# Both feed-forward products of pairs of token blocks as seven block products (Strassen) instead of eight

## The chip, the cores and the metric

The kernel runs on one core of a Trainium2 chip. Its time is the device time of one execution, in microseconds; a profile of one further execution shows what each engine did. The engines are TensorE (PE, with weight loads on PEld), VectorE (DVE), ScalarE (ACT), GpSimd (POOL) and SyncE (SP), which here issues nearly all DMA transfers. Each engine works through its own instructions in order, and waits on semaphores for the others.

## The reference

Attention with heads mixed before and after the softmax, then a feed-forward layer with the gate h - tanh(h):

```
scores = scale * np.matmul(q, k.transpose(0, 1, 3, 2))      # 8 x 12 x 448 x 448
scores = np.einsum('bhij,hg->bgij', scores, w_pre)
scores = scores - np.max(scores, axis=-1, keepdims=True)
attn = np.exp(scores)
attn = attn / (np.sum(attn, axis=-1, keepdims=True) + 1e-09)
attn = np.einsum('bhij,hg->bgij', attn, w_post)
x = np.matmul(attn, v)        # heads side by side: 3584 tokens x 768
h = x @ w_in                  # 768 x 2048
g = h - np.tanh(h)
return (g @ w_out).astype(np.float32)      # 2048 x 768
```

The weights w_in and w_out arrive as 8-byte floats.

## The kernel before

**Precision.** A product of float32 matrices is made of three matmuls in fp32r: each operand is split into a high part (the cast) and a low part (the difference), and high by high, high by low and low by high are summed in PSUM.

**Attention** (until about 854 us) goes through 180 places. A place gathers two groups of rows of scores, mixes them with w_pre (`premix`, L521), takes the maximum (DVE, L530) and the exponential (ACT, L532), and scales the post-mixing weights by the sums (`norm`: DVE L541 and L542, then POOL L543 into the tile wr). The matmuls of `mix` (L560), a place later, wait for wr. Scores, transposes and values of other rows are fitted in between by a table of due places. A generator, `narrow_steps`, adds some steps of weight conversion to each place: `narrow_chunk` (L71 to L110) turns 8-byte floats into high and low parts with operations on DVE, ACT and POOL (L96, L98, L104) and stores them in DRAM (ws). The steps are spread evenly over the places, so that POOL has the wr of each place and one or two operations of conversion between.

**Feed-forward.** The 3584 tokens are 7 blocks of 512. A block has 16 chunks of 128 hidden features. For a chunk, `hidden` multiplies 6 slices of 128 of x by w_in in 18 matmuls of 512 columns (L257, L258, L262) into one PSUM bank; `gate` and `parts_gate` make the gate from it with four passes on ACT and six on DVE, and a cast and a difference for its parts; `result` multiplies the parts by the chunk's rows of w_out, for 4 groups of 128 tokens, in 12 matmuls of 512 columns (tile ya) and 12 of 256 (yb), which add up over the 16 chunks in six banks. `hidden` of the next chunk is issued ahead of `result` of the current one, so that PE has work while the gate is made. One DMA of 1.5 MB a chunk brings the weights (tile w, a ring of six, `load_w`), and x of the next block is loaded and split during the current one, a slice every other chunk, the low part on POOL (L247).

**Order.** `in_order` chains the instructions of each engine in the order in which the program emits them. Nothing is reordered later.

## Time and profile before

| | |
|---|---|
| time, median of 3 (lowest to highest) | 1781.2 us (1780.5 to 1787.9) |
| span of the profiled execution, first to last instruction | 1783.2 us |
| attention, until about | 854 us |
| feed-forward, the rest | 929 us |
| PE / DVE / ACT / POOL busy, share of the span | 98 / 63 / 56 / 18% |
| bytes moved by DMA, mean rate | 372 MB, 209 GB/s |
| granted TensorE clock | 0.995 |

The profile gives no time of the profiled execution but its span. Busy times of matmuls overlap (the next one starts before the last has drained), so a matmul's cost is read from the distance between starts. In the groups, the number behind "idle" is the time for which the engine stood still just before these instructions, and what ended it.

### The profile page before, as it was taken

The numbers are of one execution on the slowest core, as the hardware profiler recorded it, in microseconds if no ns is written. First come the engines' busy times: TensorE is split into PE (matmuls) and PEld (weight loads), VectorE is DVE, ScalarE is ACT, GpSimd is POOL, SyncE is SP. The second block draws the span as 40 slices with busy tenths as digits, with TensorE's granted clock in tenths as the row PEclk, the third lists the DMA queues.
The fourth block names the chain that finished last, engine by engine and source line by source line (L and its number), as shares of the span: only waits on it lengthen the run. The fifth ranks groups of instructions, "written<-read, shape, count | busy, mean of one in ns | idle before, by whom it ended". The sixth has DMA issues, their size and how long they took to land.

```text
span 1783.2 us, 41383 instructions
## 1 busy us (share of the span) xinstructions
PE 1749.8 (98%) x16572; PEld 1421.2 (80%) x16572; DVE 1127.6 (63%) x2362; ACT 998.9 (56%) x2051; POOL 321.1 (18%) x417
## 2 busy tenths in 40 slices
...
GB/s 182 205 193 225 193 239 220 216 211 206 235 214 211 214 213 227 189 203 221 270 193 209 239 193 215 229 200 213 224 208 205 229 213 197 237 212 188 233 192 36
DMA packets 232816, 372.32 MB, mean 209 GB/s; under 512 B 98992, under 2 KB 207536, under 8 KB 218288
## 3 DMA queue, kind: packets, MB, share of 16 engines
...
q14 instruction: 61, 0.50, 0.1%
HBM read 245.37 MB, written 47.19 MB: 164 GB/s over the span
## 4 chain that ended last, share of the span: by engine, by line
PE 84%; DMA 5%; ACT 3%; DVE 3%; SPq 2%; issue 1%; POOL 1%; ACTq 0%; POOLq 0%; DVEq 0%
PE ps_o L560 12%; PE ps_h L257 8%; PE ps_h L258 8%; PE ps_h L262 8%; PE ps_m L602 7%; PE ps_p L521 7%; PE ya L305 6%; PE ya L302 6%; PE ya L303 6%; PE ps_q L477 5%; PE yb L305 3%; PE yb L303 3%; PE yb L302 3%; DMA t<-s 2%; SPq L369 1%
## 5 line engine op out<-in xcount | busy, mean ns | idle before, releaser
L560 PEld LDWEIGHTS ps_o<-wr,e 60*112 60x112 f32 (+1 forms) x5760 | 305.3, 175 | 34.3 <-POOL wr L543 17.2
L560 PE MATMUL ps_o<-wr,e 60*112 60x60 f32 (+1 forms) x5760 | 313.8, 258 | 8.8 <-POOL wr L543 6.7
L530 DVE TENSOR_REDUCE mx<-ps_p 128x1 f32<-128x448 f32 x360 | 207.7, 619 | 167.1 <-PE ps_p L521 166.6
L532 ACT ACTIVATE e<-ps_p,mx 128x448 f32<-128x448 f32 x360 | 225.7, 634 | 103.0 <-DVE mx L530 101.2
L289 ACT CAST gh<-r 128x512 fp32r<-128x512 f32 x112 | 69.5, 621 | 372.7 <-DVE r L282 372.7
L257 PE MATMUL ps_h<-xh,w 128*128 128x512 f32 x672 | 263.9, 393 | 0.0
L258 PE MATMUL ps_h<-xl,w 128*128 128x512 f32 x672 | 263.7, 392 | 0.0
L570 ACT COPY at<-ps_o 112x960 f32<-112x960 f32 x156 | 154.0, 987 | 92.0 <-PE ps_o L560 91.8
L521 PE MATMUL ps_p<-t,wpre 60*64 60x448 f32 (+1 forms) x1440 | 180.2, 568 | 7.7 <-DMA t<-s 7.7
L247 POOL TENSOR_TENSOR xl<-rx,xh 128x512 fp32r<-128x512 f32 x38 | 56.3, 1483 | 728.8 <-ACT xh L246 728.8
L278 DVE SCALAR_TENSOR_TENSOR r<-qa,ps_h 128x512 f32<-128x512 f32 x112 | 77.1, 689 | 158.8 <-ACT t L275 158.8
L305 PE MATMUL ya<-w,gl 128*128 128x512 f32 x448 | 176.7, 394 | 0.7 <-DVE gl L290 0.7
L302 PE MATMUL ya<-w,gh 128*128 128x512 f32 x448 | 174.9, 390 | 1.0 <-ACT gh L289 1.0
L303 PE MATMUL ya<-w,gh 128*128 128x512 f32 x448 | 174.7, 390 | 0.0
L602 PEld LDWEIGHTS ps_m<-at,vr 112*64 112x64 f32 x3072 | 147.9, 137 | 30.2 <-ACT at L577 10.4
L262 PE MATMUL ps_h<-xh,w 128*128 128x512 f32 x672 | 170.5, 389 | 0.0
L602 PE MATMUL ps_m<-at,vr 112*64 112x120 f32 (+1 forms) x3072 | 162.1, 262 | 7.4 <-ACT at L577 2.9
L272 ACT ACTIVATE u<-ps_h 128x512 f32<-128x512 f32 x112 | 67.0, 599 | 151.1 <-PE ps_h L262 151.1
L262 PEld LDWEIGHTS ps_h<-xh,w 128*128 128x128 f32 x672 | 126.1, 188 | 26.2
L258 PEld LDWEIGHTS ps_h<-xl,w 128*128 128x128 f32 x672 | 127.2, 189 | 23.6
L257 PEld LDWEIGHTS ps_h<-xh,w 128*128 128x128 f32 x672 | 127.2, 189 | 23.3
L543 POOL TENSOR_TENSOR wr<-wpost,zs 128x120 f32<-128x120 f32 x180 | 70.3, 391 | 401.3 <-DVE zs L542 302.6
...
## 6 DMA issues: line engine op xcount, KB each, us to landing
w<-ws SPq DMA_DIRECT2D x112, 1536.0 KB
...
```

The source lines that it names most:

```text
L257: nc.tensor.matmul(ph, wh[:, fs], xh, start=(c == 0), stop=False)
L258: nc.tensor.matmul(ph, wh[:, fs], xl, start=False, stop=False)
L262: nc.tensor.matmul(ph, wl[:, fs], xh, start=False, stop=(c == NK - 1))
L302: nc.tensor.matmul(y, gh[:, tok], wh[:, es], start=first, stop=False)
L303: nc.tensor.matmul(y, gh[:, tok], wl[:, es], start=False, stop=False)
L305: nc.tensor.matmul(y, gl[:, tok], wh[:, es], start=False, stop=last)
L521: nc.tensor.matmul(pss[r][halves[j], :], wpre[k, :], ts[j][k, :], start=True, stop=True)
L530: nc.vector.tensor_reduce(out=mx, in_=ps, axis=AX.X, op=ALU.max, negate=True)
L532: nc.scalar.activation(e, ps, AF.Exp, bias=mx, scale=1.0, accum_out=zs[:, 0, r : r + 1])
L560: nc.tensor.matmul(ps[:CP, j, c * GP : (c + 1) * GP].rearrange("p (h i) -> p h i", i=GI)[:, :, r * GH : (r + 1) * GH], e[k, c * CP : (c + ...
L570: nc.scalar.copy(ats[i0][:, :, :, at : at + 2 * GI].rearrange("p c h (j i) -> p j (c h) i", j=2), ps[:CP, :, : NC * GP].rearrange("p j (x ...
L602: nc.tensor.matmul(pv[j * D : (j + 1) * D, r, :n], vt[:, j, c, :], ats[i][:, c, 2 * hp + j, :n], start=(c == 0), stop=(c == NC - 1),)
```

## The change

Block 0 is computed as before. Blocks 1 to 6 are taken in three pairs, and both products of a pair are made by Strassen's scheme in Winograd's form: each matrix is cut into four quarters, and seven products of quarters (or of their sums) replace eight.

* **Weights.** `narrow_quad` converts four quarters at a time (4 x 128 columns) and also makes four sums of them: `sums_in` for w_in, `sums_out` for w_out, on POOL and one on ACT. High and low parts of quarters (wi, wo) and of sums (ss, ts) are stored in DRAM. POOL has four operations of 512 columns, and four of 128 (or one of 256 and two of 128) per quad; there are 48 quads.
* **Block 0.** `Block0.step` makes one hidden product, 18 matmuls as before; its PSUM bank is copied to SBUF by ACT, and the gate works on two chunks at once (1024 columns). The gates of block 0 are stored in DRAM (go) and read back for the result.
* **Hidden products of a pair.** `pair_step` runs eight times per pair, each for two chunks of both blocks: seven products of 9 matmuls of 512 columns, alternately in two PSUM banks X and Y. Products 2, 4 and 6 go on adding in X, and 5 in Y, with copies and sums between them on ACT and DVE (into h01 and h23). From these come two gates of 1024 columns and, a step late (`Late`), the sums of gates; one store of 7 x 512 columns (gs) puts them in DRAM.
* **Results of a pair** are made while the next pair's hidden products run. `Results` is a generator of units of 12 matmuls: for block 0 two groups of tokens as before; for a pair, one of seven products with 384 columns, which reads a gate sum from DRAM (`more_gr`), splits it (`parts`: a cast on ACT, a difference on DVE) and multiplies it by weight tiles (`more_w2`), each two or three ahead. Each step of pair 1 has 3 units, each step of pairs 2 and 3 has 5 or 6. Between two pairs stand 12 units, and after the last pair all that are left.
* **x of a pair.** Five raw quarters are loaded (`load_xq`), in the last step of the pair before; `xq_jobs` makes their four sums and all high and low parts, on ACT and DVE, 1536 columns at a time: nine jobs, for pair 1 during block 0, and for the others one with each unit between the pairs.
* The six-slot weight ring, `hidden`, `gate`, `parts_x`, `result` and the finishing functions are gone, and POOL has no work in the feed-forward but two low parts of block 0's x.

The diff, cut:

```diff
+    nc.scalar.copy(oh, m)
+    t = pool.tile([p, 4, 2, 128], F32, name="ct", tag="ct", bufs=2)
+    for job in sums(nc, m, t[:, :, 1]):
+        yield "step"
+    nc.gpsimd.tensor_sub(ol, m, raw(oh))
     yield "step"
-    nc.gpsimd.tensor_sub(fl, m, raw(fh))
+    nc.scalar.copy(t[:, :, 0].bitcast(F32R), t[:, :, 1])
+    dma(dst, raw(o).rearrange("p x t n -> p x (t n)"))
     yield "step"
-    for to, part in zip(dst, (fh, fl)):
-        if len(to.shape) == 3:
-            part = part.rearrange("p (f n) -> p f n", f=to.shape[1])
-        dma(to, raw(part))
+    nc.gpsimd.tensor_sub(t[:, :, 1].bitcast(F32R), t[:, :, 1], t[:, :, 0])
     yield "step"
+    dma(sums_dst, t.rearrange("p s t n -> p s (t n)"))
+    yield "step"
+def sums_in(nc, m, t):
+    a11, a12, a21, a22 = [m[:, x] for x in range(4)]
+    s2, s1, s3, s4 = [t[:, x] for x in range(4)]
+    nc.gpsimd.tensor_tensor(out=s1, in0=a21, in1=a22, op=ALU.add)
+    yield
+    nc.gpsimd.tensor_tensor(out=s2, in0=s1, in1=a11, op=ALU.subtract)
+    yield
+    nc.gpsimd.tensor_tensor(out=s3, in0=a11, in1=a21, op=ALU.subtract)
+    yield
+    nc.gpsimd.tensor_tensor(out=s4, in0=a12, in1=s2, op=ALU.subtract)
+    yield
+def sums_out(nc, m, t):
+    b11, b12, b21 = [m[:, x] for x in range(3)]
+    t1, t2, t3, t4 = [t[:, x] for x in (0, 1, 3, 2)]
+    both = b12.unsqueeze(1).to_broadcast([b12.shape[0], 2, b12.shape[1]])
+    nc.gpsimd.tensor_tensor(out=t[:, 0:4:3], in0=m[:, 0:4:3], in1=both, op=ALU.subtract)
+    yield
+    nc.gpsimd.tensor_tensor(out=t2, in0=b11, in1=t3, op=ALU.add)
+    yield
+    nc.gpsimd.tensor_tensor(out=t4, in0=t2, in1=b21, op=ALU.subtract)
+    yield
+    nc.scalar.mul(t2, t2, -1.0)
...
+    def load_w0(f):
+        w = ff.w0.tile([P, NK, 2, P], F32R, name="w0", tag="w0")
+        nc.sync.dma_start(raw(w), wis[f // 2][:, f % 2])
+        ff.w[f] = w
+    def products(ph, w, xs, start, stop):
+        n = len(xs)
+        for c, (xh, xl) in enumerate(xs):
+            nc.tensor.matmul(ph, w[:, c, 0], xh, start=start and c == 0, stop=False, skip_group_check=True)
+            nc.tensor.matmul(ph, w[:, c, 0], xl, start=False, stop=False, skip_group_check=True)
+        for c, (xh, _) in enumerate(xs):
+            nc.tensor.matmul(ph, w[:, c, 1], xh, start=False, stop=stop and c == n - 1, skip_group_check=True)
...
+        def a1(self):
+            self.u, self.qa = work("u"), work("qa")
+            nc.scalar.activation(self.u, self.h, AF.Square)
+            nc.scalar.activation(self.qa, self.u, AF.Square, bias=ff.bias[:, 0:1], scale=GATE_A[0])
+        def a2(self):
+            self.qb, self.t = work("qb"), work("t")
+            nc.scalar.activation(self.t, self.h, AF.Tanh)
+            nc.scalar.activation(self.qb, self.u, AF.Square, bias=ff.bias[:, 1:2], scale=GATE_B[0])
+        def d1(self):
+            nc.vector.scalar_tensor_tensor(out=self.qa, in0=self.qa, scalar=GATE_A[2], in1=self.h, op0=ALU.add, op1=ALU.mult)
+            nc.vector.tensor_sub(self.t, self.h, self.t)
+        def d2(self):
+            nc.vector.scalar_tensor_tensor(out=self.qa, in0=self.qb, scalar=GATE_B[2], in1=self.qa, op0=ALU.add, op1=ALU.mult)
+        def a3(self):
+            nc.scalar.activation(self.qb, self.u, AF.Relu, bias=ff.bias[:, 2:3], scale=1.0)
+        def d3(self, out):
+            nc.vector.tensor_mul(out, self.qa, self.u)
+            nc.vector.copy_predicated(out, self.qb.bitcast(I32), self.t)
...
+        def step(self):
+            f, old = self.f, self.old
+            self.f += 1
+            if f + 2 < NF:
+                load_w0(f + 2)
+            if f < NF:
+                ph = hbank()
+                products(ph, ff.w.pop(f), [ff.x[c] for c in range(NK)], True, True)
+                if f % 2 == 0:
+                    self.h = work(("h01", "h23")[f // 2 % 2])
+                nc.scalar.copy(self.h[:, f % 2], ph)
+            if f % 2:
+                if old:
+                    old.d2()
+                    old.a3()
+                    g = work("g", 7)[:, :2]
+                    old.d3(g)
+                    nc.sync.dma_start(gos[:, f - 3 : f - 1], g)
+                self.old = Gate(self.h) if f < NF else None
+            elif old:
+                old.a1()
+                old.a2()
+                old.d1()
...
+        def parts(self, n):
+            if n < len(self.items) and n == self.n_parts:
+                lo = ff.gr.pop(n)
+                hi = ff.gph.tile([P, 2, TB], F32R, name="gh", tag="gh")
+                nc.scalar.copy(hi, raw(lo))
+                nc.vector.tensor_sub(lo, raw(lo), raw(hi))
+                ff.gp[n] = hi, lo
+                self.n_parts += 1
...
+            first, last = new and k0 + k == 0, k0 + k == NQ - 1
+            for t in range(NT):
+                tok, y = slice(t * TT, (t + 1) * TT), self.y[t][:, :N2]
+                nc.tensor.matmul(y, gh[:, tok], wh, start=first, stop=False, skip_group_check=True)
+                nc.tensor.matmul(y, gh[:, tok], wl, start=False, stop=False, skip_group_check=True)
+                nc.tensor.matmul(y, gl[:, tok], wh, start=False, stop=last, skip_group_check=True)
...
+        def sub(x, y):
+            nc.vector.tensor_sub(xr, x if x is xr else raw(ff.xs[x]), y if y is xr else raw(ff.xs[y]))
+        def high(x, src):
+            x_tiles(x + "h")
+            nc.scalar.copy(ff.xs[x + "h"], src)
+        def low(x, src):
+            nc.vector.tensor_sub(ff.xs[x + "l"], src, raw(ff.xs[x + "h"]))
+        def both(x):
+            high(x, raw(ff.xs[x + "l"]))
+            low(x, raw(ff.xs[x + "l"]))
+        xr = ff.xr.tile([P, HK, TB], F32, name="xr", tag="xr")
+        sub("t3l", "b11l")
+        both("b11")
+        yield
+        x_tiles("t1l")
+        high("t1", xr)
+        both("b21")
+        yield
+        low("t1", xr)
+        sub("b22l", xr)
+        yield
+        x_tiles("t2l")
+        high("t2", xr)
+        low("t2", xr)
+        yield
+        sub("t4l", xr)
+        yield
+        high("t4", xr)
+        low("t4", xr)
+        yield
+        sub("b22l", "t3l")
+        yield
+        high("t3", xr)
+        low("t3", xr)
+        yield
+        both("b22")
...
+        def v0(self):
+            self.g = work("g", 7)
+            self.g2.a1()
+            self.g1.d3(self.g[:, 0:2])
+        def v1(self):
+            self.g2.a2()
+        def v2(self):
+            self.g2.d1()
+            self.g2.d2()
+        def v3(self):
+            g = self.g
+            self.g2.a3()
+            self.g2.d3(g[:, 2:4])
+            nc.vector.tensor_add(g[:, 4:6], g[:, 0:2], g[:, 2].unsqueeze(1).to_broadcast([P, 2, TB]))
+        def v4(self):
+            g = self.g
+            nc.vector.tensor_add(g[:, 6], g[:, 1], g[:, 4])
+            nc.vector.tensor_add(g[:, 2], g[:, 3], g[:, 6])
+            nc.sync.dma_start(gss[self.s][:, :, self.q], g)
+            ff.stored[self.s] = self.q + 1
...
+        X, Y = hbank(), hbank()
+        product(0, X, True)
+        h01 = work("h01")
+        nc.scalar.copy(h01[:, 1], X)
+        if late:
+            late.v0()
+        rest(0)
+        product(1, Y, True)
+        nc.vector.tensor_add(h01[:, 1], Y, h01[:, 1])
+        if late:
+            late.v1()
+        rest(1)
+        product(2, X, False)
+        if late:
+            late.v2()
+        h23 = work("h23")
+        nc.scalar.mul(h23[:, 0], X, -1.0)
+        rest(2)
+        product(3, Y, True)
+        if late:
+            late.v3()
+        nc.scalar.mul(h01[:, 0], Y, -1.0)
+        rest(3)
+        product(4, X, False)
+        nc.vector.tensor_sub(h01[:, 0], h01[:, 0], X)
+        if late:
+            late.v4()
+        g1 = Gate(h01)
+        g1.a1()
+        rest(4)
+        product(5, Y, False)
+        nc.vector.tensor_sub(h23[:, 0], h23[:, 0], Y)
+        g1.a2()
+        g1.d1()
+        rest(5)
+        product(6, X, False)
+        nc.scalar.copy(h23[:, 1], X)
+        g1.d2()
+        g1.a3()
...
+    load_all_xq(0, ("b11l", "b21l", "t3l", "b22l", "t4l"))
-    for n in range(N):
-        b, f = n // NF, n % NF
-        if n + ahead < N:
-            load_w(n + ahead)
...
+    while block0.f < NF + 2:
+        block0.step()
+        if 3 <= block0.f < NF + 1 and block0.f % 2:
+            next(xq, None)
+        if block0.f == NF - 2:
+            res.more_w2(1)
+        if block0.f == NF:
+            close_plain()
+            more_wa(6)
...
+    HELD, AHEAD = 8, 4
+    late, left = None, 4 * NQ
+    for s in range(NS):
+        per_step = (left - HELD) / NQ
+        due = 0.0
+        for p in range(NQ):
+            def between(i):
+                next(xq, None)
+                if p == NQ - 1 and s + 1 < NS:
+                    for x, at in (("b11l", 0), ("b21l", 1), ("t3l", 4), ("b22l", 5), ("t4l", 6)):
+                        if i == at:
+                            load_all_xq(s + 1, (x,))
+            units = []
+            for i in range(7):
+                due += per_step / 7
+                units.append(int(due))
+                due -= int(due)
+            late = pair_step(s, p, late, units, between)
+        left = 7 * NQ - AHEAD
+        if s + 1 < NS:
+            xq = xq_jobs()
+        for f in (late.v0, late.v1, late.v2, late.v3, late.v4):
+            f()
+            next(xq, None)
+            res.units(1)
+        late = None
+        if s + 1 < NS:
+            for _ in range(HELD + AHEAD - 5):
+                next(xq, None)
+                res.units(1)
+    for _ in res.at:
+        pass
```

428 lines of the change are left out of this document (264 added, 164 removed).

## The prediction

> **What bounds the kernel now.** I read the page's first table, then the busy time by stretches (columns: stretch and its length, then busy us and, in brackets, instructions of PE, PEld, DVE, ACT, POOL; last the granted clock, the DMA share and GB/s), cut where attention ends.
>
> ```profile
> span 1783.2 us, 41383 instructions
> ...
> PE 1749.8 (98%) x16572; PEld 1421.2 (80%) x16572; DVE 1127.6 (63%) x2362; ACT 998.9 (56%) x2051; POOL 321.1 (18%) x417
> ```
>
> ```profile
> 0.00:854.00 854.00, 826.81 (x11897) 637.93 (x11898) 586.94 (x1577) 619.02 (x1408) 267.47 (x381) 0.99 0.73 210
> 854.00:1783.00 929.00, 923.02 (x4676) 783.31 (x4675) 540.68 (x786) 379.92 (x644) 53.65 (x36) 1.00 0.58 208
> ```
>
> From 854 us on PE is busy 923 of 929 us at full clock, DVE 58% of the time, ACT 41%: the feed-forward is bound by matmuls and has room elsewhere. Before 854 us PE idles 27 us, with DVE at 69% and ACT at 72%. So matmuls taken from the second stretch shorten it, as long as the others keep up.
>
> Busy times of matmuls overlap, so their price is read from starts in order of time (start, us, what):
>
> ```profile
> 889.83 0.39 PE L302 MATMUL ya<-w,gh 128*128 128x512 f32 x1
> ...
> 892.32 0.39 PE L305 MATMUL ya<-w,gl 128*128 128x512 f32 x1
> ...
> 892.55 0.28 PE L302 MATMUL yb<-w,gh 128*128 128x256 f32 x1
> ...
> 893.86 0.28 PE L305 MATMUL yb<-w,gl 128*128 128x256 f32 x1
> ...
> 893.98 0.40 PE L257 MATMUL ps_h<-xh,w 128*128 128x512 f32 x1
> ...
> 896.50 0.39 PE L258 MATMUL ps_h<-xl,w 128*128 128x512 f32 x1
> ...
> 896.73 1.52 PE L262 MATMUL ps_h<-xh,w 128*128 128x512 f32 x6
> ...
> 898.35 0.60 ACT L272 ACTIVATE u<-ps_h 128x512 f32<-128x512 f32 x1 [0.64 <-PE ps_h L262]
> ```
>
> Each pair of rows is the first and last of 12 matmuls, 11 intervals: 2.49/11 = 0.226 us (512 columns, result), 1.31/11 = 0.119 us (256 columns), 2.52/11 = 0.229 us (512 columns, hidden). A chunk is 18 x 0.229 + 12 x 0.226 + 12 x 0.119 = 8.26 us.
>
> **What the change saves on PE.** Block 0 keeps its matmuls. A pair had 2 x 16 x 18 = 576 hidden matmuls and gets 8 steps x 7 products x 9 = 504 of the same size: 72 x 0.229 = 16.5 us, three pairs 49.5 us. Its result had 384 matmuls of 512 and 384 of 256 columns, 132.5 us; now 7 x 8 x 4 x 3 = 672 of 384 columns. No row has 384; on the line between the two it is 0.173 us (bounds 0.119 and 0.226), so 116.3 us: 16.2 us a pair, 48.7 us for three. Together **-98.2 us**.
>
> **Elementwise prices.** The gate now works on 1024 columns and the x parts on 1536; neither is in the trace. Groups of instructions (count | busy us, mean ns | idle before):
>
> ```profile
> L289 ACT CAST gh<-r 128x512 fp32r<-128x512 f32 x112 | 69.5, 621 | 372.7 <-DVE r L282 372.7
> L570 ACT COPY at<-ps_o 112x960 f32<-112x960 f32 x156 | 154.0, 987 | 92.0 <-PE ps_o L560 91.8
> L290 DVE TENSOR_TENSOR gl<-r,gh 128x512 fp32r<-128x512 f32 x112 | 78.6, 702 | 77.6 <-ACT gh L289 77.6
> L280 DVE TENSOR_TENSOR r<-r,u 128x512 f32<-128x512 f32 x112 | 109.0, 973 | 3.8
> L247 DVE TENSOR_TENSOR xl<-rx,xh 128x512 fp32r<-128x512 f32 x4 | 2.6, 684 | 1.1 <-ACT xh L246 1.1
> L429 DVE TENSOR_TENSOR kk<-ps_k,kk 128x448 fp32r<-128x448 f32 x2 | 1.1, 616 | 0.0
> ```
>
> DVE: (684 - 616)/64 = 1.06 ns a column, so 1.23 us for 1024 and 1.77 us for 1536. ACT: (987 - 621)/448 = 0.82 ns, so 1.04 and 1.46 us. L280 is dearer than its like; in order of time:
>
> ```profile
> 893.50 1.64 POOL L247 TENSOR_TENSOR xl<-rx,xh 128x512 fp32r<-128x512 f32 x1 [12.23 <-ACT xh L246]
> ...
> 894.02 1.66 DVE L280 TENSOR_TENSOR r<-r,u 128x512 f32<-128x512 f32 x1
> ```
>
> It ends 0.54 us after POOL's, so about 0.7 us of it are its own work: beside POOL it is held up. The new feed-forward gives POOL nothing to do, so I use the undisturbed price. The Trainium skill (SBUF — State Buffer, "SBUF: two separate sides") gives this as a lock: a DVE operation with two SBUF inputs and a GpSimd one that reads SBUF exclude each other for the whole instruction. The trace agrees with the row above; with L280's 0.97 us for all two-input work the next term would be some 28 us larger.
>
> **The gaps between pairs: +48 us.** In a step of pair 1 PE has 63 x 0.229 = 14.4 us of hidden and 3 units of result (12 matmuls, 2.08 us each): 20.7 us; in pairs 2 and 3 5.5 units, 25.9 us. DVE per step: two gates of 5 operations of 1024 (12.3), gate sums 1 of 1024 and 2 of 512 (2.6), three PSUM sums (2.1), parts of stored gates 0.75 to 2.75 x 1.23 (0.9 to 3.4): 18 to 20.4 us. It fits. Between two pairs, though, PE has 12 units, 25 us, while DVE must finish the last gates and make the next pair's x parts. Before, x came a chunk at a time, on POOL. DVE, one whole chunk of the feed-forward before (far, r, t are gate tiles, gl the low part of the finished gate):
>
> ```order
> L277 TENSOR_SCALAR far<-u 128x512
> L278 SCALAR_TENSOR_TENSOR r<-qa,ps_h 128x512
> L279 SCALAR_TENSOR_TENSOR r<-qb,r 128x512
> L280 TENSOR_TENSOR r<-r,u 128x512
> L281 TENSOR_TENSOR t<-ps_h,t 128x512
> L282 COPY_PREDICATED r<-far,t 128x512
> L290 TENSOR_TENSOR gl<-r,gh 128x512
> ```
>
> and now, the second half of the first gap (g is the tile of gates and their sums; b, t and xr are parts of x; gl a gate read back for the result, the last row those of the last units):
>
> ```order
> L638 TENSOR_TENSOR g<-g 128x1024
> L568 TENSOR_TENSOR t2l<-xr,t2h 128x1536
> L642 TENSOR_TENSOR g<-g 128x512
> L643 TENSOR_TENSOR g<-g 128x512
> L561 TENSOR_TENSOR xr<-t4l,xr 128x1536
> L438 TENSOR_TENSOR gl<-gl,gh 128x1024
> L568 TENSOR_TENSOR t4l<-xr,t4h 128x1536
> L561 TENSOR_TENSOR xr<-b22l,t3l 128x1536
> L568 TENSOR_TENSOR t3l<-xr,t3h 128x1536
> L568 TENSOR_TENSOR b22l<-b22l,b22h 128x1536
> L438 TENSOR_TENSOR gl<-gl,gh 128x1024 x2
> ```
>
> What moved: a whole pair's x parts now stand ahead of the gate parts that PE waits for. Counted from the gap's start there are 11 of 1536 (19.5 us), 11 of 1024 up to the first of the last two (13.5) and 2 of 512 (1.4): 34.4 us, against 10 units = 20.8 us on PE, so PE waits 13.6 us. On ACT the high parts (7 x 1.46 us) stand in line with Squares and Tanh, and DVE's next row needs them: the one for b21 comes some 3 us late, the four differences each cost up to 1.5: I add 8, 22 us. The second gap has two parts and eight sums more, 2.5 + 8 x 0.55 = 7 on DVE, some of it inside ACT's waits: 26 us. Bounds: 34 (no wait for ACT) and 70 (every cast waited for, 2 x 7 x 1.46, and handovers).
>
> **Other stalls in the feed-forward.** (a) Pair 1's x, 3.9 MB, is now issued on SP ahead of hidden product 3's weights:
>
> ```profile
> 851.42 0.50 PE L257 MATMUL ps_h<-xh,w 128*128 128x512 f32 x1
> 854.89 0.57 SPq L369 DMA_DIRECT2D xs<-x  x1
> 859.78 0.40 PE L257 MATMUL ps_h<-xh,w 128*128 128x512 f32 x1
> ```
>
> SP where attention's last output goes out, before (w_N is one feature chunk's weights, xs_N attention's output, rx raw x):
>
> ```order
> L369 DMA xs_64<-x 768x1x208
> L334 DMA w_13209<-ws_65 128x3072
> L334 DMA w_13211<-ws_66 128x3072
> L334 DMA w_13213<-ws_66 128x3072
> L334 DMA w_13284<-ws_66 128x3072
> L334 DMA w_13349<-ws_66 128x3072
> L238 DMA rx<-xs_58 128x384
> ```
>
> and now (b11l to t4l are the five raw quarters of pair 1's x, the last row the weights of hidden product 3):
>
> ```order
> L738 DMA xs_64<-x 768x1x208
> L556 DMA b11l<-xs_58 128x3x384
> L556 DMA b11l<-xs_59 128x3x128
> L556 DMA b21l<-xs_58 128x3x384
> L556 DMA b21l<-xs_59 128x3x128
> L556 DMA t3l<-xs_59 128x3x320
> L556 DMA t3l<-xs_60 128x3x192
> L556 DMA b22l<-xs_59 128x3x320
> L556 DMA b22l<-xs_60 128x3x192
> L556 DMA t4l<-xs_58 128x3x384
> L556 DMA t4l<-xs_59 128x3x128
> L308 DMA w_13433<-wi_66 128x1536
> ```
>
> What moved: ten x transfers got between the last output and those weights, which were in SBUF or first in line before. And product 3 comes sooner, with hidden products 1 and 2 alone ahead of it: 851.4 + 2 x 4.1 = 859.7. The DMA rows by stretch of one chunk:
>
> ```profile
> 866.25:874.50 8.25, 8.25 (x44) 7.06 (x43) 4.53 (x7) 3.03 (x6) 0.00 (x0) 1.00 1.01 426
> 899.25:907.50 8.25, 8.25 (x43) 7.06 (x42) 4.49 (x8) 2.97 (x6) 0.00 (x0) 1.00 0.52 186
> 400.00:500.00 100.00, 98.11 (x1456) 76.22 (x1454) 73.15 (x196) 76.57 (x174) 34.94 (x44) 1.00 0.80 225
> ```
>
> The saturated rate is 426 GB/s: 4.7 MB take 11 us from 854.9, so PE waits **6 us** (0 if attention's end leaves SP free sooner, 12 at 281 GB/s). The Trainium skill (DMA: Bandwidth & Descriptors, "Where 436 GB/s comes from") has about 358 GB/s of HBM as the limit of a core; the row is above it. By that page this would be 13 us, the stall 8.
>
> (b) Pair 1's first weights are loaded over block 0's last ones, so PE waits for one whole DMA of 0.39 MB; the nearest row, of the chain of waits (start, us), is of a 0.2 MB one:
>
> ```profile
> 21.95 3.53 DMA t<-s
> ```
>
> I take 3.5 us (bounds 1, at 426 GB/s, and 8). (c) In pairs 2 and 3 three steps each end without a result unit, and the next product reuses the PSUM bank just filled: a copy like L272, from 898.35 to 898.95, where the next matmul would start at 898.1: 1.0 us x 6 = 6 us. (d) Block 0: DVE needs 5 x 1.23 + 19.5/7 = 8.9 us per two products of 8.2 on PE: 5 us; waits of the single gate-sum tile for its store, closings of products: 3. Together 8 (0 to 35, the latter if that store holds each step of pair 1 for 4 us).
>
> Transfers otherwise hide: a step of pairs 2 and 3 moves 7 weight tiles of 0.39 MB, 1.84 MB of gates to DRAM, and 2.75 times 0.79 MB of weights and 0.52 MB of gates back, 8.2 MB in 25.9 us or 317 GB/s; a step of pair 1 6.2 MB in 20.7 us.
>
> **Attention: +12 us.** POOL rows (by form), and PE's wait:
>
> ```profile
> L98 POOL TENSOR_TENSOR cm<-cm,cr 128x512 f32<-128x512 f32 x24 | 31.8, 1325 | 0.7
> L543 POOL TENSOR_TENSOR wr<-wpost,zs 128x120 f32<-128x120 f32 x180 | 70.3, 391 | 401.3 <-DVE zs L542 302.6 <-PE ps_o L560 49.0 <-PE ps_p L521 19.7
> L560 PEld LDWEIGHTS ps_o<-wr,e 60*112 60x112 f32 (+1 forms) x5760 | 305.3, 175 | 34.3 <-POOL wr L543 17.2 <-issue 8.6 <-POOL cl L104 1.3
> ```
>
> POOL in the middle of attention before (wr is what each mix on PE waits for, the others convert weights):
>
> ```order
> L543 TENSOR_TENSOR wr<-wpost,zs 128x2x60
> L96 TENSOR_TENSOR cm<-cr,cs 128x512
> L98 TENSOR_TENSOR cm<-cm,cr 128x512
> L543 TENSOR_TENSOR wr<-wpost,zs 128x2x60
> L104 TENSOR_TENSOR cl<-cm,cs 128x512
> ```
>
> and now (co the parts of a weight, ct those of its sums):
>
> ```order
> L912 TENSOR_TENSOR wr<-wpost,zs 128x2x60
> L97 TENSOR_TENSOR cm<-cr,co 128x512
> L110 TENSOR_TENSOR ct<-ct 128x4x128
> L99 TENSOR_TENSOR cm<-cm,cr 128x512
> L912 TENSOR_TENSOR wr<-wpost,zs 128x2x60
> L120 TENSOR_TENSOR ct<-cm 128x128
> L122 TENSOR_TENSOR ct<-ct,cm 128x128
> L124 TENSOR_TENSOR ct<-cm 128x128
> L126 TENSOR_TENSOR ct<-cm,ct 128x128
> ```
>
> What moved: up to four conversions, where one or two stood, are ahead of a wr. They cost POOL 192 us before (56 x 3 operations); now 48 x 4 x 1.3 + about 48 x 1.6 for the sums = 327, +135. 854 us in 180 places is 4.7 us a place, and 0.4 + 2.0 us fit; but rows like L110 wait for ACT and hold wr. PE's 17 us for wr, scaled by 327/192, become 29: +12. Bounds 0 and 68, half of what is added.
>
> **Sum.** -98.2 + 48 + 6 + 3.5 + 6 + 8 + 12 = -14.7: the profiled 1783.2 becomes 1768.5. The shown median, 1781.2, lies 2.0 below that execution, so **1766**; 1745 to 1800 if this account holds.
>
> **Rivals.** A: DVE is no limit in the gaps, and POOL no limit before: without those 60 us, 1706. For it: DVE 58% busy. Against: the 34 us counted. B, slower: POOL in order holds wr. Its price is half the added 135 us, 68 instead of 12: 1822. It decides where a place's POOL rows outlast the place: the one quoted has 0.4 + 3.9 us of 4.7, plus waits. Against: most wr wait for zs now (303 of 401 us). C: transfers get only attention's rate, 225/0.80 = 281 GB/s; late steps then take 29.2 us, 16 x 3.3 = 53, pair 1's 8 x 1.3 = 10, and the closing results (1.31 MB per 4.16 us of PE) 30 x 0.5 = 15: 1844. Against: 426 was reached; for it: 1 to 3 KB rows.
>
> **Chances.** Forecast 0.55, A 0.17, B 0.16, C 0.12. This kernel's measurement tells about 0.5% (1772 to 1790) from no change. Faster: A and two thirds of the forecast, 0.53; same 0.18; slower: B, C and a little, 0.29. The range 1708 to 1818 leaves out C and the ends of A and B.
>
> **What would show it.** PE idle of 15 to 30 us twice, some 200 us apart, ended by DVE's gl; an idle of about 6 us four products into the feed-forward, ended by a weight DMA; hidden and result spacing unchanged, 0.17 us for 384 columns; POOL near 410 us, PE's wait for wr near 30. Wrong if PE is full in the gaps (A), if the first stretch passes 900 us (B), or the DMA share sits at 1.0 through the late steps (C).

## The result: 3% slower

The changed kernel takes 1837.0 us (median of 4, 1836.7 to 1841.2) against 1783.6 for the kernel before beside it: a ratio of 1.031 (95% interval 1.028 to 1.035). Forecast were 1766 and a range of 1708 to 1818; the time lies outside, on the other side of 1781.

Busy time by stretches, the changed kernel's profile first. The columns are those of the prediction's first such view; the cuts are, in order, attention, block 0, pair 1, gap 1, pair 2, gap 2, pair 3 and the rest (the "tail"):

```profile
0.00:870.30 870.30, 826.72 (x11773) 636.98 (x11773) 583.59 (x1530) 644.06 (x1449) 402.46 (x572) 0.98 0.79 232
870.30:986.30 116.00, 80.52 (x387) 64.23 (x385) 63.53 (x52) 57.52 (x63) 1.51 (x3) 0.82 0.52 180
986.30:1160.30 174.00, 167.99 (x781) 139.25 (x782) 132.80 (x128) 105.52 (x115) 0.00 (x0) 0.97 0.78 283
1160.30:1214.00 53.70, 32.98 (x156) 29.49 (x155) 36.88 (x27) 24.74 (x31) 0.00 (x0) 0.81 0.79 281
1214.00:1420.80 206.80, 206.80 (x1024) 185.35 (x1023) 148.49 (x144) 123.43 (x143) 0.00 (x0) 1.00 0.86 314
1420.80:1471.50 50.70, 30.70 (x144) 28.38 (x143) 40.23 (x35) 21.84 (x19) 0.00 (x0) 0.83 0.79 281
1471.50:1678.30 206.80, 206.80 (x1024) 185.35 (x1023) 147.97 (x143) 123.18 (x143) 0.00 (x0) 1.00 0.82 301
1678.30:1839.40 161.10, 144.12 (x792) 141.76 (x791) 61.97 (x64) 47.76 (x55) 0.00 (x0) 0.96 0.85 303
```

The kernel before, cut where its feed-forward starts, which is at about 842 us and not at the 854 that stand ahead of the prediction:

```profile
0.00:842.20 842.20, 815.01 (x11773) 628.05 (x11774) 582.74 (x1570) 615.25 (x1401) 264.89 (x379) 0.99 0.74 211
842.20:1783.20 941.00, 934.82 (x4800) 793.19 (x4799) 544.88 (x793) 383.69 (x651) 56.23 (x39) 1.00 0.57 207
```

Pairs 2 and 3 are what was forecast: 206.8 us for 8 steps, 25.85 a step, TensorE (PE) never idle, full clock. Everything between is not. Block 0 has 288 matmuls of 0.229 us, 66 us (with 96 small ones of attention's end the stretch comes to 70), and takes 116. And the granted clock, the last but two number, is 0.81 to 0.83 in block 0 and the gaps and 0.96 to 0.98 in attention, pair 1 and the tail; before the change it was 1.00 through the feed-forward.

So each stretch has three parts: matmuls at full speed, idle time, and what the half clock costs. The last I work out from the trace's records as half of the time in which PE was busy while the granted clock stood at 0.5.

| us | length | idle | lost at half clock | full speed |
|---|---|---|---|---|
| before: attention | 841.8 | 27.2 | 6.9 | 807.7 |
| before: feed-forward | 941.4 | 6.2 | 1.6 | 933.6 |
| after: attention | 870.3 | 43.6 | 17.4 | 809.3 |
| after: feed-forward | 969.2 | 99.2 | 29.8 | 840.2 |
| of it block 0 | 116.0 | 35.5 | 10.3 | 70.2 |
| pair 1 | 174.0 | 6.0 | 3.9 | 164.1 |
| the two gaps | 104.5 | 40.7 | 10.0 | 53.8 |
| tail | 161.2 | 17.0 | 5.5 | 138.6 |

The scheme's saving is there: 933.6 to 840.2, 93.4 us. It is eaten by 93.0 us of new idle and 28.2 us of half clock in the feed-forward, and attention adds 28.5. Where the five longest idles of PE in the feed-forward ended (PE in order of time; the bracket gives the idle before the row and what ended it):

```profile
898.58 0.77 PE L315 MATMUL ps_h<-xh,w 128*128 128x512 f32 x1 [10.17 <-DMA w<-wi]
...
928.90 0.77 PE L315 MATMUL ps_h<-xh,w 128*128 128x512 f32 x1 [5.88 <-DMA w<-wi]
...
986.27 0.76 PE L315 MATMUL ps_h<-b11h,wa 128*128 128x512 f32 x1 [13.49 <-DMA wa<-wi]
...
1203.47 0.66 PE L523 MATMUL y<-w,gh 128*128 128x384 f32 x1 [13.61 <-DMA w<-wo]
...
1431.61 0.66 PE L523 MATMUL y<-w,gh 128*128 128x384 f32 x1 [8.74 <-ACT qb L337]
```

Four of the five end with a load of weights. Those loads are issued by SP, and SP waits for something else (its own waits: us in total, times, longest):

```profile
SPq L644 <- DVE g L643: 158.0, 23, 20.2
...
SPq L377 <- DVE g L351: 79.1, 8, 16.6
```

L644 and L377 are the stores of gates to DRAM. Each stands in SP's queue until VectorE (DVE) has made the gate, and the loads behind it stand too. The theories to be told apart: **order on SP** (those stores), **DVE's work** (the x parts make the gates late, SP only shows it), **the clock** (idles cost more than themselves), and for attention **GpSimd's sums** against transfers.

### The profile page after: what moved, and what is told of

It is laid out like the page before. It is cut to its first block, busy times and chain, and to the rows that moved or that the text cites. A ratio compares the mean times of both kernels' runs of the same rounds, so it can differ in the third digit from the quotient of the medians.

```text
span 1839.4 us, 40980 instructions
## 1 busy us (share of the span) xinstructions
PE 1696.6 (92%) x16068; PEld 1410.8 (77%) x16068; DVE 1215.5 (66%) x2119; ACT 1148.1 (62%) x2016; POOL 404.0 (22%) x574
## 4 chain that ended last, share of the span: by engine, by line
PE 67%; DMA 12%; DVE 8%; ACT 6%; issue 3%; POOL 2%; SPq 2%; ACTq 0%; DVEq 0%; POOLq 0%
PE ps_o L929 12%; PE ps_m L971 8%; PE ps_p L890 7%; PE ps_h L315 6%; PE ps_h L316 6%; PE ps_h L318 5%; PE y L523 5%; PE ps_q L846 5%; PE y L525 5%; PE y L524 5%; DMA t<-s 2%; DMA gs<-g 2%; DMA w<-wo 1%; DMA vr<-in_v_dram 1%; PE ps_m L812 1%
## 5 line engine op out<-in xcount | busy, mean ns | idle before, releaser
L929 PEld LDWEIGHTS ps_o<-wr,e 60*112 60x112 f32 (+1 forms) x5760 | 307.7, 176 | 42.8 <-POOL wr L912 18.4
L523 PE MATMUL y<-w,gh 128*128 128x384 f32 x672 | 231.6, 345 | 39.8 <-DMA w<-wo 20.0
L525 PE MATMUL y<-w,gl 128*128 128x384 f32 x672 | 230.8, 343 | 7.2 <-DVE gl L438 7.2
L524 PE MATMUL y<-w,gh 128*128 128x384 f32 x672 | 230.0, 342 | 0.0
L438 DVE TENSOR_TENSOR gl<-gl,gh 128x1024 fp32r<-128x1024 f32 x92 | 112.6, 1224 | 172.3 <-ACT gh L437 172.2
L523 PEld LDWEIGHTS y<-w,gh 128*128 128x128 f32 x672 | 130.0, 193 | 46.6 <-ACT b22h L565 13.8
L437 ACT CAST gh<-gl 128x1024 fp32r<-128x1024 f32 x92 | 96.0, 1044 | 110.5 <-DMA gl<-gs 78.3
L525 PEld LDWEIGHTS y<-w,gl 128*128 128x128 f32 x672 | 129.8, 193 | 8.7 <-DVE gl L438 8.6
L524 PEld LDWEIGHTS y<-w,gh 128*128 128x128 f32 x672 | 129.9, 193 | 3.7
L846 PE MATMUL ps_q<-kk,qh 64*120 64x448 f32 (+1 forms) x768 | 123.7, 399 | 1.2 <-DVE kk L798 0.5
L846 PEld LDWEIGHTS ps_q<-kk,qh 64*120 64x120 f32 (+1 forms) x768 | 59.9, 176 | 82.8 <-issue 51.4
L851 DVE COPY s<-ps_q 120x448 f32<-120x448 f32 (+1 forms) x192 | 112.5, 615 | 11.9 <-PE ps_q L846 10.6
L347 ACT ACTIVATE qb<-u,bias 128x1024 f32<-128x1024 f32 x56 | 64.7, 1155 | 68.4 <-DVE qa L344 68.2
```

The lines of the kernel that those rows point to most:

```text
L438: nc.vector.tensor_sub(lo, raw(lo), raw(hi))
L523: nc.tensor.matmul(y, gh[:, tok], wh, start=first, stop=False, skip_group_check=True)
L524: nc.tensor.matmul(y, gh[:, tok], wl, start=False, stop=False, skip_group_check=True)
L525: nc.tensor.matmul(y, gl[:, tok], wh, start=False, stop=last, skip_group_check=True)
L846: nc.tensor.matmul(ps[:n, :S], qx[a, hp, :], kx[a, hp % 2], start=(x == 0), stop=(x == 2))
L851: eng(sts[i][:n, 2 * hp + j, :], ps[:n, :S])
```

## The experiments

### Stalls filled with small products

```diff
+            if f in (3, 8, 12):
+                fill({3: 40, 8: 22, 12: 20}[f])
```

`fill(n)` issues n products of 64x64 zeros. The same was done ahead of pair 1, in the gaps and after pair 3 (not shown).

> Ten of the longest stalls of TensorE in the feed-forward (three in block 0, one before pair 1, three in the first gap, two in the second, two after pair 3; 73 us of idle) are filled to some 70% with small products on zeros (64x64, results thrown away) placed right ahead of the instruction that waits. What the instruction waits for does not change. Theory 'clock' (an idle of over 1 us of TensorE is followed by 3.4 to 13.7 us at half clock, and that costs time of its own): the half-clock time of the feed-forward falls from about 99 to under 50 us and the run gets 15 to 40 us shorter, 1797 to 1822. Rival 'what is waited for sets the time' (the half clock only stretches work that would wait afterwards anyway, for VectorE or for loads): 1830 to 1842, with the idle moved behind the fills.

1831.9 us, 1.0275 (1.0251 to 1.0299). The feed-forward went from 969.2 to 965.7 us. 35 us of idle became 35 us of small products, but the loss at half clock only fell from 29.8 to 26.8, since the idles that were left, 1.2 to 6 us each, drew windows of half clock of their own. So this run doesn't price the clock. It does show that the time of block 0 (111.1 us for 116.0) is set by what PE waits for, as the rival said. The clock had to be tested where PE sets the time (the forced waits, below).

### The gates' stores on GpSimd's queue

```diff
-                    nc.sync.dma_start(gos[:, f - 3 : f - 1], g)
+                    nc.gpsimd.dma_start(gos[:, f - 3 : f - 1], g)
...
-            nc.sync.dma_start(gss[self.s][:, :, self.q], g)
+            nc.gpsimd.dma_start(gss[self.s][:, :, self.q], g)
```

> The 8 stores of block 0's gates and the 24 of gates and sums are issued by GpSimd's queue in place of SP's; nothing else is changed. Theory 'SP in order' (a store that waits for VectorE's late gate holds the loads queued behind it, which TensorE needs): the idles at block 0 (5.9 and 5.1 us), before pair 1 (13.5) and in the first gap (13.6), all ended by a load of weights, go to under 3 us each, with their half-clock windows: 40 to 60 us shorter, 1780 to 1797. Rival 'VectorE in the gaps' (the parts of the next x make the gate and everything after it late, SP only shows it): only block 0's two idles go; 1815 to 1832, and the first gap's idle stays over 15 us in all.

1900.6 us, 1.065 (1.062 to 1.069): 69 us above the higher of the two forecast ranges. Block 0 did shorten, 116.0 to 95.1, and its idles of 5.9 and 5.1 us went. But the steps of the pairs stalled: pair 1 took 207.1 us for 174.0. The issues of this kernel (KB each, median us to landing):

```profile
gs<-g POOLq DMA_DIRECT2D x24, 1792.0 KB, 11.4
```

and DVE within a step of pair 1:

```profile
1093.68 1.22 DVE L344 SCALAR_TENSOR_TENSOR qa<-qb,qa 128x1024 f32<-128x1024 f32 x1
1104.09 1.22 DVE L350 TENSOR_TENSOR g<-qa,u 128x1024 f32<-128x1024 f32 x1 [9.19 <-DMA gs<-g]
```

There is one tile g for the seven gates and sums of a step. Over this queue its store lands 11.4 us after the issue, DVE waits 9.2 us to write the next gate, and the PSUM sums behind it hold PE. With SP's stores that wait is 3.3 us at most. The queue as such could thus not be tested alone. The gaps (54.6 and 49.4 us) stayed as they were, but this run doesn't say why: the late landings may have taken back what the order gave.

### No x parts in the gaps

```diff
-                if p == NQ - 1 and s + 1 < NS:
+                if False:
                     for x, at in (("b11l", 0), ("b21l", 1), ("t3l", 4), ("b22l", 5), ("t4l", 6)):
...
-        if s + 1 < NS:
-            xq = xq_jobs()
```

> Left out: the loads and the high and low parts of x for pairs 2 and 3, which reuse those of pair 1 (blocks 3 to 6 of the output are another's); all else stays. Per gap VectorE has 11 operations of 1.75 us less (19 us) and ScalarE 7 of 1.47. Theory 'VectorE in the gaps': both gaps' idles (34 and 20 us, with windows at half clock behind them) nearly go: 45 to 75 us shorter, 1764 to 1795. Theory 'SP in order': the first gap's 13.6 us stays at 8 or more because the store still waits for a gate that is made in the gap; 20 to 35 us shorter, 1804 to 1820.

1808.3 us, 1.014 (1.012 to 1.016): 29 us less, inside the range of the theory "SP in order" and 13 us short of the other's. By stretches, gap 1 and gap 2, and the row of PE behind gap 1's longest idle:

```profile
1154.60:1197.20 42.60, 30.11 (x157) 27.23 (x156) 18.38 (x17) 15.33 (x24) 0.00 (x0) 0.84 0.84 300
1404.00:1440.10 36.10, 28.62 (x144) 27.10 (x143) 21.76 (x24) 12.09 (x12) 0.00 (x0) 0.91 0.89 314
```

```profile
1186.46 0.66 PE L523 MATMUL y<-w,gh 128*128 128x384 f32 x1 [10.49 <-DMA w<-wo]
```

Taking 18.5 us of work a gap off DVE shortens the gaps by 11.1 and 14.6 us. In gap 2 that is most of the idle (20.0 to 7.5 us). In gap 1, 12.5 of 20.7 us stay, and 10.5 of them are the wait for the same load that took 13.6 before: it still goes out behind the store of a gate that is made in the gap. So by this run order on SP is the larger part in gap 1, and DVE's work in gap 2.

### Block 0 mended

```diff
-                    g = work("g", 7)[:, :2]
+                    g = raw(ff.gpl.tile([P, 2, TB], F32R, name="gl", tag="gl"))
...
-                    nc.sync.dma_start(gos[:, f - 3 : f - 1], g)
+                    self.held.append((f, g))
...
-    load_all_xq(0, ("b11l", "b21l", "t3l", "b22l", "t4l"))
+        for x, at in (("b11l", 2), ("t3l", 2), ("b21l", 3), ("b22l", 4), ("t4l", 5)):
+            if block0.f == at:
+                load_all_xq(0, (x,))
-        if 3 <= block0.f < NF + 1 and block0.f % 2:
+        if 5 <= block0.f < NF + 1 and block0.f % 2:
             next(xq, None)
```

The gates in `held` are stored two products later, behind the loads; the last two lines start the jobs of x one pair of products later.

> Block 0 alone is changed: its gates go into the three tiles that later hold gates read back (one tile of its own before), each store is issued by SP two products later, behind the loads that are due sooner, and the five x loads of pair 1 go out one by one after products 2 to 5 and not all ahead of product 3's weights; the jobs of x start one pair of products later. What VectorE and ScalarE do is the same. Theory 'order on SP and one gate tile': block 0's 116 us (65.7 at full speed) fall to 75 to 88, its idle from 35 to under 12, total 1800 to 1812. Rival 'VectorE's work' (71 us of operations that wait for one another through ScalarE): block 0 stays at 98 or more, total 1822 to 1835.

1818.7 us, 1.021 (1.017 to 1.025), between the two ranges. Block 0 and pair 1:

```profile
875.30:962.20 86.90, 74.71 (x387) 59.30 (x385) 52.58 (x44) 51.28 (x57) 1.57 (x3) 0.95 0.67 233
962.20:1144.00 181.80, 171.61 (x781) 141.57 (x782) 143.65 (x136) 111.29 (x121) 0.00 (x0) 0.95 0.77 274
```

Block 0 fell by 29 us, to what the first theory gave (75 to 88). No work is left out, but 11 us of DVE's and 6 of ScalarE's (ACT's) moved on into pair 1, which grew by 8 us. Over both stretches 21 us are gone at the same work: that much was order on SP, the single gate tile and the place of the x jobs, which this run doesn't tell apart.

### Gaps mended

```diff
+                if i in (3, 5):
+                    next(ahead[1], None)
...
-            xq = xq_jobs()
+            xq = ahead[1]
+        n_gap = 2
```

The first two jobs of x (b11 and t1) are made in the pair's last step, two (b21 and t2) in the gap, the rest in the next pair's first step.

> The gaps between pairs alone are changed: of the parts of the next x, b11 and t1 are made in the pair's last step (B12 is loaded a second time for it), b21 and t2 in the gap, t4, t3 and b22 in the first step of the next pair; the gap's last store of gates is issued three result units later. The work is the same but for two loads of 0.8 MB. Theory 'VectorE's queue in the gaps': 7 of 19 us of it stay in the gap, and the gaps (54 and 51 us) come to 36 to 44, as without any x parts (43 and 36): total 1808 to 1822. Rival 'the work only moves' (the step that takes it up stalls as much): the gaps shrink but pair 2 and 3 grow by as much, total 1830 to 1842.

1829.2 us, 1.024 (1.020 to 1.028). Gap 1, pair 2, gap 2, pair 3:

```profile
1168.60:1205.90 37.30, 30.61 (x156) 27.34 (x156) 23.63 (x19) 18.06 (x26) 0.00 (x0) 0.91 0.95 337
1205.90:1417.80 211.90, 207.65 (x1023) 185.06 (x1023) 159.45 (x150) 128.75 (x147) 0.00 (x0) 1.00 0.87 317
1417.80:1462.80 45.00, 28.99 (x145) 27.75 (x144) 30.92 (x30) 17.41 (x17) 0.00 (x0) 0.85 0.87 308
1462.80:1673.70 210.90, 207.76 (x1023) 184.99 (x1022) 156.09 (x148) 126.65 (x146) 0.00 (x0) 1.00 0.82 302
```

The gaps lose 22 us, and the two pairs that take the work up gain 9: half of each theory.

### Both mendings

> The changes of the two runs before this one together. If the two stalls are independent, the gains add: 1837 less 30 less 22, 1778 to 1795, level with the kernel before or a little over. If one feeds the other (block 0's lateness is carried into pair 1), less than the sum: over 1800.

1816.8 us, 1.018 (1.015 to 1.021): over 1800, as the second theory had it, but not for its reason. In the feed-forward the two mendings gained 16.6 and 8.8 us alone, and together 27.5: the gains add. What is missing had gone to the neighbouring pairs in each run already. The profile shows a reason for it, which the next run tests. ACT and DVE of this kernel, a part of block 0 (us, length, what; each engine works in the order shown):

```profile
940.58 1.47 ACT L571 CAST t2h<-xr 128x1536 fp32r<-128x1536 f32 x1 [2.10 <-DVE xr L567]
941.96 0.58 ACT L376 COPY h<-ps_h 128x512 f32<-128x512 f32 x1
945.08 1.15 ACT L347 ACTIVATE qb<-u,bias 128x1024 f32<-128x1024 f32 x1 [2.54 <-DVE qa L344]
```

```profile
938.80 1.75 DVE L567 TENSOR_TENSOR xr<-b22l,xr 128x1536 f32<-128x1536 f32 x1
942.09 1.76 DVE L574 TENSOR_TENSOR t2l<-xr,t2h 128x1536 fp32r<-128x1536 f32 x1 [1.54 <-ACT t2h L571]
943.76 1.22 DVE L344 SCALAR_TENSOR_TENSOR qa<-qb,qa 128x1024 f32<-128x1024 f32 x1
```

DVE makes a sum of x; ACT, which stood waiting, casts it; DVE, which stood waiting, subtracts; ACT stands again until DVE has come to the gate's product. Neither is full (DVE 11.1 of 15 us, ACT 10.3), but each waits for the other's last instruction, and the copy that frees PE's PSUM bank (L376) stands in that row.

### The hand-overs taken apart

Block 0 mended as above, and: the gate's last DVE product is issued with the first two; each x part is cut into stages of one operation an engine, one stage a product; result units go ahead of gate and x work.

```diff
                 old.a1()
                 old.a2()
                 old.d1()
+                old.d2()
...
-        both("b11")
-        yield
+        high("b11", raw(ff.xs["b11l"]))
+        yield
+        low("b11", raw(ff.xs["b11l"]))
```

> Block 0 as in the run that mended it alone, and besides: in block 0 the gate's last VectorE product is issued with the first two, so that ScalarE's relu a product later finds it done; every x part is cut into stages of one operation on an engine, one stage a product, so that none waits for the stage just ahead of it; four stages in a pair's last step, seven in the gap, three in the next pair's first step; in the gaps and steps a result unit goes ahead of the gate and x work in VectorE's queue (it ends with the copies that free PSUM banks); the first weights of pair 1 lie over the w0 tile that comes free first; gap and tail store their gates later. Theory 'the order in which ScalarE and VectorE hand over to each other is the price': feed-forward (969 us now, 942 with both mendings) at 895 to 922: block 0 70 to 80, gaps 28 to 36, tail 145 to 152. Total 1765 to 1790 with attention at 868. Rival 'their total work is the price' (VectorE 68 us of work in block 0's 66, 26 in a gap of 25): 930 or more.

1782.4 us, 0.999 (0.997 to 1.001) of the kernel before. The feed-forward is 914.3 us, 55 less than in the changed kernel, with the same work on PE, DVE and ACT. Block 0, pair 1 and the gaps:

```profile
861.60:940.40 78.80, 71.89 (x386) 58.24 (x385) 55.32 (x46) 53.07 (x58) 1.50 (x3) 0.98 0.74 258
940.40:1117.30 176.90, 169.31 (x781) 139.50 (x782) 140.47 (x133) 110.12 (x119) 0.00 (x0) 0.97 0.79 284
1117.30:1156.40 39.10, 30.45 (x156) 27.18 (x156) 30.97 (x25) 20.85 (x28) 0.00 (x0) 0.87 0.94 336
...
1365.10:1409.20 44.10, 31.51 (x146) 29.93 (x145) 34.77 (x32) 17.05 (x17) 0.00 (x0) 0.85 0.97 355
```

So 55 of the feed-forward's 121 us of idle and half clock beyond the kernel before were order: one half went with both mendings (942 us), the other with this run's edits (914). The gaps (39 and 44, forecast 28 to 36) and the tail (160, forecast 145 to 152) missed their numbers; in the gaps DVE has 31 and 35 us of work beside 27 and 26 of PE at full speed.

### Forced waits where PE sets the time

```diff
+        if s:
+            z = ff.bias[:, 4:]
+            for _ in range((0, 3, 9)[s]):
+                nc.scalar.copy(z, X[:, :60])
+            nc.tensor.matmul(Y[:60, :60], z, z, start=True, stop=True)
```

> In pairs 2 and 3 of the changed kernel, where TensorE is never idle and sets the time (207 us each), each of the 8 steps gets one forced wait after its first product: a chain of 3 small ScalarE copies in pair 2, of 9 in pair 3, which a small product waits for. Theory 'half clock costs half where TensorE sets the time': each idle of over about 1 us draws a window of 3.4 us or more at half clock, and the pair grows by its idle plus half of its half-clock time: with 8 x 3 us and 8 x 3.4 us at half, pair 3 grows by 24 + 14 = 38; pair 2 with 8 x 1 us by 8 to 22. Rival 'an idle costs only itself': by 24 and 8.

Pairs 2 and 3 by stretches:

```profile
1220.50:1442.00 221.50, 210.77 (x1038) 185.96 (x1038) 148.58 (x144) 127.04 (x167) 0.00 (x0) 1.00 0.82 295
1490.80:1735.80 245.00, 222.41 (x1039) 196.77 (x1038) 148.19 (x144) 137.14 (x215) 0.00 (x0) 0.94 0.71 256
```

PE's waits in pair 3:

```profile
PE ps_h L669 <- ACT bias L668: 22.6, 8, 3.3
```

Pair 2 had seven idles of 1.27 us and one of 1.85, 10.7 in all. The clock stayed at 1.00, and the pair grew by 14.7: the idle and 4.0 us of the small products (busy 206.8 to 210.8). Pair 3 had eight of 2.7 to 3.3 us, 22.6 in all. The clock fell for 27.3 us, and the pair grew by 38.2: idle, 4.0, and 11.6 more of busy time for the same matmuls. So idles of 1.3 us cost themselves, and those of 2.7 to 3.3 us half as much again on average, which is the clock theory's number for pair 3 (38). It had half clock begin at idles of about 1 us, and there was none after 1.3. These times are of one execution.

But only six of these eight were followed by half clock. The longest, 3.31 us up to 1526.24, was not; one of 2.85 us up to 1554.60 was. In the trace's record of the clock, all windows of half clock start on one grid of 3.41 us. The two idles by stretches of that grid:

```profile
1521.27:1524.68 3.41, 1.66 (x8) 1.01 (x6) 2.28 (x2) 3.35 (x9) 0.00 (x0) 1.00 0.85 296
1524.68:1528.09 3.41, 1.85 (x11) 1.78 (x12) 0.00 (x0) 3.19 (x9) 0.00 (x0) 1.00 0.54 215
1551.99:1555.40 3.41, 0.80 (x5) 0.74 (x6) 2.52 (x2) 3.16 (x12) 0.00 (x0) 1.00 1.02 421
1555.40:1558.82 3.42, 3.42 (x12) 3.35 (x11) 0.00 (x0) 3.39 (x5) 0.00 (x0) 0.50 0.60 237
```

The first idle lies across a border, 1.75 and 1.56 us; the second has 2.61 us in one stretch, and the next runs at half clock. In the feed-forwards of all 16 profiles, every stretch of the grid at full clock with more than 2.0 us of idle was followed by one at half clock, and none with less than 1.6 us. The Trainium skill (TensorE: Matmul & The Clock Gate, "Part 1: The HAM clock gate (the "warmup" mystery)") has the clock halve after at least one idle window of about 3.4 us. The trace agrees with the length of a window (3.41 us, or twice that), but idles shorter than one were enough here.

### Attention: without the sums, and without their stores

```diff
-    for job in sums(nc, m, t[:, :, 1]):
+    for _ in range(4 if sums is sums_in else 3):
         yield "step"
...
-    nc.scalar.copy(t[:, :, 0].bitcast(F32R), t[:, :, 1])
...
-    nc.gpsimd.tensor_sub(t[:, :, 1].bitcast(F32R), t[:, :, 1], t[:, :, 0])
...
-    dma(sums_dst, t.rearrange("p s t n -> p s (t n)"))
+    dma(sums_dst, raw(o).rearrange("p x t n -> p x (t n)"))
```

> Left out in attention: the sums of the weights' quarters and their split (three to four small and one large operation of GpSimd and one copy of ScalarE per conversion); the store that carried them sends the same number of bytes of the parts instead, so that the transfers are as many and as large (the sums that the feed-forward reads are wrong). Theory 'GpSimd holds wr': attention ends 20 to 28 us earlier, at 842 to 850 in place of 870, total 1811 to 1820. Rival 'the added transfers (18 MB more written) or the conversions' slots': attention ends at 865 to 870 as now, total 1832 to 1842.

1826.9 us, 1.026 (1.021 to 1.032); attention ended at 863.2, between the two ranges. Without the stores too (the `dma` of the sums is cut as well):

> As the run without the sums, and their stores (48 of 512 KB, 25 MB in attention) are left out too; the feed-forward reads other parts of the weights of the same size in their place. Attention then has the conversions of before, but in quads of four quarter rows. Theory 'the added transfers': attention ends at 843 to 850 (863 without the sums alone, 860 to 870 with them). Rival 'the conversions' new order and their slots': 856 or more. Total 20 to 27 us below the changed kernel in the first case, about 10 in the second.

1824.7 us, 1.022 (1.019 to 1.025); attention ended at 856.5, which is the rival's number (856 or more, some 10 us less in all). By these times work and transfers together are worth some 12 us, and attention stays 15 us above the kernel before's 841.8. How far half clock hides more is taken up below.

### Attention: ACT eased

PE's longest waits in attention, before and after the change:

```profile
PE ps_p L521 <- DMA t<-s: 7.7, 8, 1.7
PE ps_o L560 <- POOL wr L543: 6.7, 11, 1.2
PE ps_m L602 <- ACT at L577: 2.9, 4, 1.0
PE ps_m L602 <- ACT at L570: 2.5, 4, 1.9
```

```profile
PE ps_p L890 <- DMA t<-s: 11.0, 10, 3.7
PE ps_o L929 <- ACT at L939: 7.0, 9, 1.4
PE ps_m L971 <- ACT at L946: 5.2, 6, 2.8
PE ps_o L929 <- POOL wr L912: 4.9, 8, 1.2
```

The prediction took PE's wait for wr from the weight loads' row (17.2 us before). That row after the change:

```profile
L929 PEld LDWEIGHTS ps_o<-wr,e 60*112 60x112 f32 (+1 forms) x5760 | 307.7, 176 | 42.8 <-POOL wr L912 18.4
```

So the wait for wr hardly moved (17.2 to 18.4 on PEld, 6.7 to 4.9 on PE). The waits of PE for `at`, ACT's copies of mixed weights, grew from 6.8 to 14.5 us in all. ACT waits 23.3 us for GpSimd with a conversion's copy at its head (0.6 before):

```profile
ACT co L101 <- POOL cm L99: 23.3, 19, 3.4
```

```diff
     yield "step"
+    yield "step"
+    yield "step"
     nc.scalar.copy(oh, m)
```

> One edit in attention: in a weight's conversion ScalarE's copy of the high part is issued two conversion steps after GpSimd's sum that it reads, not right behind it. In the changed kernel ScalarE waits 23.3 us for that sum (19 times; 0.6 us before the change), and TensorE's waits for at, ScalarE's copy behind it, grew from 6.8 to 14.5 us, while its waits for wr fell from 6.7 to 4.9. Theory 'ScalarE held by the conversion': the 23 us go under 5, and attention ends 8 to 16 us earlier, at 852 to 862; total 1821 to 1829. Rival 'GpSimd's work and transfers': attention at 863 to 873, total 1832 to 1842.

1827.1 us, 1.025 (1.022 to 1.027), 10 us better than the change and inside the theory's range; attention ended at 859.3, and ACT's wait fell to 7.0 us (above the 5 expected). But the wait moved on:

```profile
PE ps_o L931 <- POOL wr L914: 11.2, 16, 1.6
```

So I left the sums out of this kernel as well:

> The conversion steps of the run that eased ScalarE in attention, with the sums' work on GpSimd and ScalarE left out as in the earlier run without sums (the same bytes are stored; the sums read later are wrong). With ScalarE eased, TensorE's waits for wr rose from 4.9 to 11.2 us. Theory 'GpSimd holds wr once ScalarE doesn't': those waits fall to 6 or less and attention ends at 845 to 853 (859 with the sums). Rival 'transfers and the gathers behind them are what is left': 856 to 862.

1836.3 us, 1.030 (1.028 to 1.033): no gain at all, and attention at 869.6, above both ranges, with 45 us of busy time at half clock. The wait for wr fell to 7.0 us only (6 expected). Each of the two edits gained some 10 us alone, and nothing together. What this stretch loses depends on where its small idles fall, and the grid of the clock starts elsewhere in each profile. Nine of the profiled kernels have the changed kernel's attention instruction for instruction, and it ended between 860.1 us (27.3 us busy at half clock) and 879.3 (65.6):

```profile
0.00:879.30 879.30, 840.04 (x11773) 645.17 (x11773) 586.18 (x1530) 645.10 (x1449) 403.35 (x573) 0.96 0.77 230
```

With half of that time taken off, all nine end between 844.8 and 852.9; the kernel before, so reckoned, at 834.9. So reckoned, the kernels with ACT eased (this one's forerunner and the two below) end at 846.3 to 852.7, this one at 847.1, the one without the sums at 843.9, and the one without their stores as well at 836.6. Easing ACT thus shows no gain beyond the spread, and of all these edits only leaving out the stores brings attention back to within 2 us of the kernel before. That speaks for the added transfers; it is one profile against a spread of 8 us, and not shown.

### All mendings, and one more round

> The mended feed-forward and the mended attention together. If both hold and add: 1752 to 1782, faster than the kernel before. If the feed-forward's work is the price or attention does not move: 1785 to 1810.

1779.0 us, 0.9968 (0.9950 to 0.9986): the feed-forward at 912.4 us, attention at 860.1. It is the fastest here, 0.3% below the kernel before, with the interval just under 1; for use that is no gain.

> The mended kernel (feed-forward and attention), with three more places where an instruction stands ahead of one that is due sooner: block 0's stores are held four products, so that pair 1's first weights are not behind one (5.7 us of idle); block 0's last gate is issued inside pair 1's first step, behind the copies that free its PSUM banks (3.4 us); each gap and the tail begin with two result units ahead of the gate work (4.7 us twice), and the stage that reads b22 comes one unit later (its load is waited for 3.2 us). Theory 'order': 8 to 20 us below the mended kernel's 1779, 1759 to 1771. Rival 'the work of VectorE and ScalarE': the idle moves to the next product, 1774 to 1784.

1781.2 us, 0.9994 (0.9975 to 1.0014). Block 0 came to 75.3 us, 5 above the stretch's work at full speed, but pair 1 took the gain back (177.7 to 181.5) and the gaps grew by 1 and 3 us. The rival holds for this round: the idle moved to the next product. The feed-forward still loses some 66 us more than the kernel before's to idle and half clock. In the gaps DVE has 31 us of work beside PE's 28, so its work is the likely cause there; the rest was not taken further apart.

## Why the prediction was wrong

From the forecast's 1768.5 to the measured span of 1839.4 are 70.9 us. By its own terms, idle and half clock together:

| term | forecast | measured | difference |
|---|---|---|---|
| matmuls in the feed-forward | -98.2 | -93.4 | +4.8 |
| attention | +12 | +28.5 | +16.5 |
| (a), (b), (d): block 0, pair 1's start | +17.5 | 45.8 in block 0, 9.9 in pair 1 | +38.2 |
| gaps | +48 | 26.4 and 24.3 | +2.7 |
| (c) bank hand-over in pairs 2 and 3 | +6 | 0 | -6 |
| tail | none | 22.5 | +22.5 |
| lost already before the change | | -7.8 | -7.8 |

**Right.** The matmuls (25.85 us a step, 25.9 forecast). The elementwise prices. GpSimd's 404 us (410). The sizes of the two gaps (50.7 us, 48 forecast), but in part by luck: 10 of the 50.7 are half clock, which the term didn't have, and the cause that it gave, DVE's x parts, holds for gap 2 alone. Without them half of the excess went, and in gap 1 the wait for a load behind a gate's store stayed. The sign that I gave, long idles ended by DVE's gl, didn't come: the two longest ended with that load and with ACT. Rival C fell: pairs 2 and 3 ran at 301 to 314 GB/s without one idle.

**The step that failed most is (a) to (d) as one.** I priced block 0 as a sum of work (8.9 us of DVE against 8.2 of PE) and single loads, each beside a free queue. I named the store of the single gate tile, and bounded it at 35 us, but as a hold on pair 1's steps. What I didn't ask is what stands behind the waiting store on SP: the next weights. The run that mended block 0 took 29 us of its 46 away and gave 8 back in pair 1, with no work left out; the run that also took the hand-overs between ACT and DVE apart saved 34 us over both stretches. (a), 6 us with bounds 0 and 12, was 10.2; (b), 3.5 with an upper bound of 8, was 13.5, since its load stood behind such a store.

**The tail** was left out: after pair 3 the same gate work and the same store come, with 17.0 us of idle and 5.5 of half clock.

**The clock** was missing from every term. Each idle was priced at itself; the loss to half clock grew by 38.7 us, 28.2 of them in the feed-forward and 10.5 in attention. The profile of before had what was needed: its rows showed clock 1.00 where PE was full and 0.99 in attention with its short idles. I wrote idles of 15 to 30 us into the sum without asking what they do to the clock.

**Attention: the mechanism was wrong.** I scaled PE's wait for wr, 17 us, to 29 by GpSimd's work; that work came as forecast, and the wait is 18.4. What grew in the trace are the waits for ACT, held by a conversion that waits for GpSimd, those for transfers, and half clock. Rival C's 1844 is the number nearest to the result, which is luck: nothing of its mechanism came. Rival B (1822) has the mechanism that failed here. How the 28.5 us divide stays open: 16.4 are idle and 10.5 half clock, but the edits that took single causes away did not add up, and with half clock taken off, only the run without the sums and their stores lies clearly outside the spread of 8 us.
